# A written-out order of tasks, laid out anew: the first two layers of an attention and expert kernel, and which elementwise work GpSimd takes

## The chip, the cores and the metric

The kernel runs on one core of one Trainium2 chip. The metric is device time in microseconds of one execution, the median of several. The core's engines each run their own queue of instructions in order: PE (TensorE, matmuls; PEld is its loading of weights), DVE (VectorE), ACT (ScalarE), POOL (GpSimd), and SP (SyncE), which here only issues DMAs. An instruction whose input is not ready holds up everything behind it on its engine.

## The reference, cut to what matters

```python
# batch 4, heads 8, sequence 576, head width 64, 32 memory slots; all float32
a = softmax over the sequence of phi                      # (b, h, s, m)
k_m, v_m = a^T k, a^T v                                   # 32 memory rows per head
attn = softmax over m of (q k_m^T / 8)
x = (attn v_m), heads side by side                        # 2304 tokens x 512
h = x @ w_in                                              # 512 -> 2048
x = (max(h, 0) + alpha * min(h, 0)) @ w_out               # 2048 -> 512
p = domain_probs / (their sum + 1e-9)                     # 4 experts
out = sum over e of p[:, e] * (max(x @ w1[e], 0) @ w2[e]) # 512 -> 1024 -> 512
```

The weights w_in and w_out come as float64 and are decoded on the chip. "The first layers" below are the attention and the layer of w_in and w_out; the experts follow.

## The kernel before, in words

**Stages.** The attention of a batch `b` has two halves `g` of the heads (tasks `a{b}{g}_...`: the softmax of phi, its transposes on PE, the memory products, the scores, and their way back from PSUM) and a second softmax (`s{b}{g}{offset}_...`, class `Soft`, L364): `max`, `sub`, `exp`, `sum`, `mul`, `back`, then a split into a high and a low part, `hi` and `lo`. Batch 0 does it in two pieces of 288 columns, the others in one of 576. Then come 128 steps j of the first dense layer (class `First`, L542): for each of four blocks of 512 hidden columns, each batch, each half of 288 tokens, four pieces of 128 hidden columns. A step's tasks are `u{j}` (the up product on PE, L559 or L562), `n{j}` (two activations on ACT, L575 and L576), `v{j}` (DVE, L581), `h{j}` and `l{j}` (split into a high part on ACT, L585, and a low part, L232 on DVE or POOL), `d{j}` (the down product on PE, L597 or L600), and after four steps `e{j}` (the sum in PSUM goes to SBUF, L611 or L613). The first eight steps (batch 0, first block) are in plain float32 and have no `h` and `l`; the rest makes three float32r products of the high and low parts. `f{b}{c}{e}` folds the values of the attention into a piece of w_in on PE (L523), `fh` and `fl` split the result.

**Weights.** A block of w_in or w_out (`in{i}`, `out{i}`, class `Decode`, L442) is loaded into one of three buffers and decoded in steps: `_0` (DVE, L459), `_1` (ACT, L463), `_2` (DVE, L469 and L470), `_3` (L477, always DVE here), `_4` (the add, L496, DVE or POOL) and, for `out`, `_5` and `_6` (high part on ACT, low part on DVE or POOL, L232). The task `_3` also issues the load of a later block on SP (L438). SP's other loads, `p{b}`, `q{b}`, `kv{b}`, are tasks too, so their place in the order is their place in the queue of transfers. `w{i}` are idle matmuls that fill PE's early gaps.

**What sets the order.** The text ORDER names all tasks of the first layers in one sequence. They are issued in it, each to its own engine's queue; nothing is reordered afterwards, and the waits between engines follow from the data. The set ON_VECTOR names the tasks whose elementwise operation goes to DVE rather than POOL. `Soft` asks it once for both `sub` and `mul` (under the name of `sub`), and once for `lo`:

```python
 228     def engine(name):
 229         return nc.vector if name in ON_VECTOR else nc.gpsimd
...
 372         def views(self):
 373             s = pe_t[self.b][:, S2 + self.g * S + self.o:S2 + self.g * S + self.o + self.n]
...
 382         def sub(self):
 383             s, s3, shape = self.views()
 384             mx = self.mx
 385             self.eng.tensor_tensor(out=s3, in0=s3, in1=mx.to_broadcast(shape), op=ALU.subtract)
...
 399         def mul(self):
 400             s, s3, shape = self.views()
 401             rs = self.rs
 402             self.eng.tensor_tensor(out=s3, in0=s3, in1=rs.to_broadcast(shape), op=ALU.mult)
```

`Decode` asks it under `_3`, `_4` and, in the split, `_6`:

```python
 449 
 450         def open(self):
...
 472         def third(self):
 473             s = self.s.bitcast(F32)
 474             if self.eng is nc.gpsimd:
 475                 nc.gpsimd.tensor_tensor(out=s, in0=self.low.bitcast(F32), in1=s, op=ALU.mult)
 476             else:
 477                 nc.vector.scalar_tensor_tensor(out=s, in0=self.low, scalar=2.0**-52, in1=s, op0=ALU.mult, op1=ALU.mult)
 478             if n_raw[0] < n_dense + 2:
 479                 load_raw()
```

After ORDER has run, `run_experts` (L844) issues the experts in loops over 32 units of block and batch, by a fixed program that the change does not touch. Its first DMAs are the loads of the gates, `p<-pd` (L719), which stand on SP behind the task `sp3` (a store of batch 3's result, L625).

Of the kernel before, what the change touches and what calls it, by code (L numbers as in the profile page):

```python
# [1108 lines left out]
```

## Time and profile before

| | |
|---|---|
| time, median of 3 runs (lowest, highest) | 1208.26 us (1206.77, 1208.98) |
| the profiled execution's own time | 1206.66 us |
| its span, first to last instruction | 1204.7 us |
| mean granted TensorE clock over the span | 0.990 |
| busy: PE / PEld / DVE / ACT / POOL | 1170.1 / 1123.2 / 782.4 / 468.0 / 420.2 us |
| first layers, about | 0 to 418 us |
| experts, about | 418 to 1205 us |

The profile is that of one execution. Busy times are averages over stages that differ, so they are read stage by stage: the busy time of the engines in windows of the span, then the chain of work that ended last (followed back from the end, at each step to what released it), then the groups of instructions with count and mean duration. The two numbers ahead of a row of the timeline are its start and its duration, and the square bracket at its end is the engine's idle time before it and what ended that.

### The profile page before, as it was taken

Reading aid. Unit: us, or ns where it says so; the run is one execution under the profiler, and the core shown is the slowest. Engines: PE = TensorE matmul, PEld = TensorE weight load, DVE = VectorE, ACT = ScalarE, POOL = GpSimd, SP = SyncE. Lnnn points to the kernel's source line nnn. Section 1 sums busy time; section 2 is a strip of 40 time slices with the busy share of each in tenths; the row PEclk is TensorE's granted clock in tenths of the full one; section 3 lists DMA queues with packets and bytes.
Section 4 is the critical chain, followed back from the end, with each engine's and each line's share of the span. In section 5 each row is a group of like instructions: output and inputs, shape, how many; then the busy total and the mean of one; then the engine's idle time right before and its main releaser. Section 6 shows DMA issues by size and latency. Waiting matters only on the chain.

```text
span 1204.7 us, 21401 instructions
## 1 busy us (share of the span) xinstructions
PE 1170.1 (97%) x8794; PEld 1123.2 (93%) x8794; DVE 782.4 (65%) x1433; ACT 468.0 (39%) x1017; POOL 420.2 (35%) x361
## 2 busy tenths in 40 slices
PE   7799999999999989999999999989999999999998
PEld 6478899998999989999999999989999999999998
DVE  6999997685457744555566566676456656656553
ACT  4557665545455533323232223233422223232320
POOL 2212111232000054444534435465443552553430
PEclk9899999999999999999999999989999999999999
DMA  9642122010000132111112111132112111111001
GB/s 376 250 160 83 54 87 71 19 53 18 1 1 1 56 97 92 55 54 53 46 48 69 37 54 36 64 124 75 53 47 62 54 46 45 58 41 63 36 29 70
DMA packets 22994, 82.46 MB, mean 68 GB/s; under 512 B 3312, under 2 KB 4336, under 8 KB 20976
## 3 DMA queue, kind: packets, MB, share of 16 engines
q1 hardware_dynamic: 22896, 81.09, 19.8%
...
## 4 chain that ended last, share of the span: by engine, by line
PE 87%; DVE 9%; DMA 2%; ACT 1%; issue 1%; SPq 0%; ACTq 0%; DVEq 0%
PE o L823 34%; PE y L600 14%; PE uy L732 12%; PE uw L732 8%; PE ux L732 8%; PE h L562 7%; PE pw L523 2%; DMA rawin<-in_w_in 2%; PE y L597 1%; DVE g L232 1%; DVE xt L660 1%; DVE pos L581 1%; DMA p<-pd 1%; DVE min L469 0%; DVE mout L469 0%
## 5 line engine op out<-in xcount | busy, mean ns | idle before, releaser
L823 PE MATMUL o<-g,w 128*128 128x288 f32 x3072 | 450.9, 296 | 1.1 <-DVE g L232 1.1
L823 PEld LDWEIGHTS o<-g,w 128*128 128x128 f32 x3072 | 423.2, 189 | 1.8 <-DVE g L232 1.6
L232 POOL TENSOR_TENSOR w<-raww,w 128x512 fp32r<-128x512 f32 (+1 forms) x96 | 150.3, 1580 | 260.4 <-ACT w L507 155.3
L835 DVE TENSOR_TENSOR acc<-o,acc 128x288 f32<-128x288 f32 x224 | 102.1, 456 | 189.0 <-PE o L823 189.0
L600 PE MATMUL y<-g,wout 128*128 128x288 f32 x1440 | 210.1, 298 | 2.6 <-DVE g L232 1.0
L600 PEld LDWEIGHTS y<-g,wout 128*128 128x128 f32 x1440 | 195.9, 188 | 12.6 <-ACT pos L576 4.2
L732 PE MATMUL uy<-x,w 128*128 128x288 f32 x1152 | 186.0, 297 | 8.0 <-DVE v L766 8.0
L732 PEld LDWEIGHTS uy<-x,w 128*128 128x128 f32 x1152 | 164.7, 189 | 9.4 <-DVE v L766 9.3
L770 ACT COPY v<-ux 128x288 f32<-128x288 f32 x64 | 25.6, 400 | 291.8 <-PE ux L732 288.5
L801 ACT CAST g<-h 128x576 fp32r<-128x576 f32 x128 | 83.3, 676 | 139.5 <-DVE h L795 139.5
L232 POOL TENSOR_TENSOR g<-h,g 128x576 fp32r<-128x576 f32 x64 | 92.8, 1451 | 127.8 <-ACT g L801 123.0
L732 PE MATMUL ux<-x,w 128*128 128x288 f32 x768 | 123.4, 296 | 2.5 <-ACT v L770 2.5
L732 PE MATMUL uw<-x,w 128*128 128x288 f32 x768 | 123.1, 296 | 0.1
L795 DVE SCALAR_TENSOR_TENSOR h<-h,p 128x576 f32<-128x576 f32 x128 | 109.4, 855 | 6.4 <-DMA p<-pd 3.3
L562 PE MATMUL h<-a,wp 128*128 128x288 f32 x720 | 111.6, 297 | 0.3
L732 PEld LDWEIGHTS ux<-x,w 128*128 128x128 f32 x768 | 109.3, 189 | 2.7 <-ACT v L770 2.7
L732 PEld LDWEIGHTS uw<-x,w 128*128 128x128 f32 x768 | 109.3, 189 | 0.3 <-DVE y L611 0.3
L562 PEld LDWEIGHTS h<-a,wp 128*128 128x128 f32 x720 | 100.0, 188 | 5.3 <-issue 3.0
L766 DVE TENSOR_TENSOR v<-uy,v 128x288 f32<-128x288 f32 x128 | 58.5, 457 | 69.9 <-PE uy L732 69.4
L581 DVE SCALAR_TENSOR_TENSOR pos<-neg,nal,pos 128x288 f32<-128x288 f32 x120 | 64.7, 542 | 58.3 <-ACT pos L576 57.8
L575 ACT ACTIVATE neg<-h 128x288 f32<-128x288 f32 x128 | 52.8, 413 | 83.1 <-PE h L562 76.3
L232 POOL TENSOR_TENSOR g<-pos,g 128x288 fp32r<-128x288 f32 x24 | 19.7, 823 | 182.7 <-ACT g L585 134.2
(116 smaller groups left out, 1184.3 us busy)
## 6 DMA issues: line engine op xcount, KB each, us to landing
...
```

The lines of the kernel that those rows point to most:

```text
L232: eng.tensor_tensor(out=out, in0=in0, in1=in1.bitcast(F32), op=ALU.subtract)
L562: mm(p, wp_t[b, c, f // 2][:, x, o2 + g * 256:o2 + g * 256 + 128], a_t[b][:, y, g, o:o + HB], start=(n == 0), stop=(n == 5))
L575: nc.scalar.activation(out=neg, in_=p, func=AF.Relu, scale=-1.0)
L581: nc.vector.scalar_tensor_tensor(out=pos, in0=neg, scalar=nal[:, ft:ft + 1], in1=pos, op0=ALU.mult, op1=ALU.add)
L600: mm(First.acc[d], w[:, x, d * 128:(d + 1) * 128], self.gt[:, y, 0:HB], start=(self.start and n == 0), stop=(self.stop and n == 2))
L732: mm(p, w[:, x, a, k], operand(self.b, i)[:, y, k], start=(start and n == 0), stop=(n == 5), skip_group_check=not start)
L766: nc.vector.tensor_tensor(out=out, in0=x, in1=y, op=ALU.add)
L770: nc.scalar.copy(out=self.v1_t, in_=self.x)
L795: nc.vector.scalar_tensor_tensor(out=h, in0=h, scalar=0.0, in1=p_t[self.g // 2, self.b], op0=ALU.max, op1=ALU.mult)
L801: nc.scalar.copy(out=g_t[self.g, self.b, self.hp][:, i, 0], in_=h)
L823: mm(self.p, w[:, x, i, d % 2 * 128:(d % 2 + 1) * 128], g, start=(m == 0), stop=(m == 11))
L835: nc.vector.tensor_tensor(out=a, in0=self.p, in1=a, op=ALU.add)
```

## The change

It replaces the text of ORDER and the set ON_VECTOR. No task's own work is changed. The weights' adds of the first blocks, and other halves of the second softmax, go to POOL; other `lo`, `_4`, `_6` and `l` tasks change engine in either direction. The loads of `q1`, `p2` and `kv2` change place among the weights' loads. The numbers of idle matmuls change, and the fifth group (`w4`) is gone. Cut below: ORDER from its start until past step 24, and its end; ON_VECTOR whole.

```diff
 ORDER = """
-w0 p0 pal ppr kv0 pr0 pr1 pr2 q0 w1 p1 kv1 q1 a00_max a01_max a00_exp a01_exp a00_nat a00_sum a00_natc a01_nat a01_sum
-  pgates a01_nath a01_natc w2 a01_nathc a01_mem in0_1 in0_0 a00_mem in0_2 a01_memc in1_1 in0_3 out0_1 in1_0 in1_2
-  a01_memt a00_memc q01 p2 a01_memtc a00_memt out0_0 in1_3 a01_sc0 a00_memtc out0_2 q2 a00_sc0 a01_ev0 in0_4 w3 a00_ev0
-  s010_max in1_4 s000_max s010_sub f000 a10_max s000_sub s010_exp a11_max w4 fh000 out0_3 s000_exp a10_exp s010_sum
-  out0_4 a11_exp s000_sum a10_nat s010_mul a10_sum a10_natc a11_nat s000_mul s010_back a11_nath a11_natc a11_sum
-  a11_nathc s000_back in2_1 u0 out0_5 in2_0 u1 n0 in2_2 a00_sc1 n1 in2_3 a01_sc1 v0 in2_4 in3_1 d0
-v1 in3_0 in3_2 in3_3 in3_4 a01_ev1 out0_6 out1_1 a00_ev1 f001 s01288_max out1_0 out2_1 a10_mem out1_2 fh001 out3_1
-  out1_3 s000_hi out1_4 u2 a10_memc kv2 out2_0 d1
-n2 out2_2 out1_5 out2_3 s010_hi a11_mem s00288_max in4_1 out2_4 out3_0 out2_5 v2 s00288_sub d2
-s01288_sub s00288_exp out3_2 s01288_exp a11_memc out1_6 s00288_sum u3 s01288_sum a10_memt out2_6 n3 a20_max a11_memt
-  a10_memtc out3_3 a11_memtc a10_sc1 a20_exp s00288_mul p3 s01288_mul a10_sc0 out3_4 in5_1 v3 out3_5 s010_lo s01288_back
-  d3
-s00288_back s01288_hi out3_6 s00288_hi a10_ev0 s000_lo in6_1 u4 a10_ev1 e3 s01288_lo a11_sc1 s00288_lo s100_max s100_sub
-  n4 a11_sc0 a11_ev1 s100_exp v4 u5 a11_ev0 d4
-s110_max n5 s110_sub s100_sum s110_exp u6 f100 v5 n6 s110_sum d5
-fh100 s100_mul s110_mul u7 s100_back f101 q3 v6 s100_hi s110_back n7 d6
-pst s100_lo s110_hi fl100 fh101 s110_lo a20_nat a21_max u8 v7 a21_exp u9 fl101 d7
-n8 a20_sum a21_sum a20_natc v8 n9 in4_0 a21_nat h8 v9 a21_nath e7 l8 u10 in4_2 a21_natc d8
-in4_3 a21_nathc in5_0 h9 in5_2 a20_mem n10 l9 v10 in5_3 h10 a21_mem l10 a20_memc in6_0 a31_max in4_4 a31_exp in6_2 d9
-kv3 a21_memc in5_4 a30_max in7_1 u11 a31_sum a30_exp in6_3 a20_memt n11 a30_sum in6_4 a21_memt a20_memtc d10
-a21_memtc v11 out4_1 in7_0 a20_sc0 h11 in7_2 a20_sc1 a20_ev0 l11 u12 a20_ev1 s200_max a21_sc1 n12 s200_sub a21_sc0
-  a21_ev1 s200_exp v12 d11
-out5_1 a21_ev0 h12 s210_max l12 u13 s200_sum e11 s210_sub u14 d12
-n13 s200_mul s210_exp v13 f200 s210_sum h13 n14 l13 u15 s200_back fh200 s210_mul d13
-fl200 s200_hi n15 v14 f201 s200_lo s210_back h14 s210_hi a30_nat l14 a30_natc s210_lo d14
-fh201 v15 fl201 h15 u16 l15 in7_3 d15
-n16 out4_0 v16 out4_2 a31_nat h16 e15 a31_nath l16 u17 out4_3 a31_natc d16
-out5_0 in7_4 a31_nathc n17 out4_4 a30_mem out4_5 v17 out5_2 h17 out6_1 l17 out5_3 a31_mem a30_memc out4_6 out6_0 out7_1
-  out5_4 out6_2 u18 a31_memc d17
-n18 out6_3 out5_5 v18 u19 h18 out5_6 a30_memt l18 n19 out7_0 a31_memt a30_memtc v19 d18
-a31_memtc out6_4 h19 out7_2 out6_5 a30_sc1 in8_1 l19 out7_3 a30_sc0 a30_ev1 out6_6 u20 a30_ev0 s300_max out7_4 a31_sc0
-  n20 in9_1 a31_sc1 a31_ev0 out7_5 s300_sub d19
-a31_ev1 out7_6 s300_exp s310_max u21 v20 e19 s310_sub u22 s300_sum f300 h20 n21 l20 f301 s310_exp v21 h21 d20
-s310_sum n22 l21 fh300 s300_mul d21
-fh301 s310_mul in10_1 s300_back u23 v22 s300_hi s310_back h22 s300_lo s310_hi l22 n23 s310_lo d22
-fl300 v23 u24 fl301 h23 n24 u25 l23 in8_0 d23
-n25 v24 in8_2 h24 u26 e23 l24 v25 u27 in8_3 d24
-h25 in9_0 n26 l25 in9_2 n27 d25
...
-x1l1 n124 x1h2 v124 u125 h124 e123 l124 n125 u126 n126 d124
-v125 x1l2 h125 l125 u127 v126 d125
-n127 h126 v127 x1h5 l126 h127 d126
-x1l5 x1h6 l127 to wh01 x1l6 d127
+w0 p0 pal ppr kv0 pr0 pr1 pr2 w1 q0 p1 kv1 a01_max q01 a00_max a01_exp a00_exp a01_nat a01_sum pgates a00_nat a00_sum
+  a01_natc a01_nath a00_natc w2 a01_nathc a01_mem in0_1 in0_0 in0_2 a00_mem a01_memc in1_1 in1_0 out0_1 in1_2 a01_memt
+  a00_memc in0_3 a01_memtc a00_memt out0_0 a01_sc0 a00_memtc in1_3 a00_sc0 a01_ev0 in0_4 w3 a00_ev0 q1 s010_max p2
+  s000_max kv2 s010_sub a11_max s000_sub a10_max s010_exp a11_exp s010_sum in1_4 s000_exp a11_nat a10_exp s010_mul
+  s000_sum f000 s010_back a11_natc s000_mul a10_nat a11_sum fh000 a11_nath s000_back a10_natc out0_2 u0 a11_nathc
+  a01_sc1 out0_3 n0 a00_sc1 a01_ev1 out0_4 in2_1 u1 q2 a00_ev1 s01288_max in3_1 in2_0 a11_mem n1 s00288_max s01288_sub
+  a10_sum s00288_sub s01288_exp in2_2 s00288_exp a10_mem a11_memc in3_0 out0_5 in3_2 a11_memt a10_memc in2_3 a11_memtc
+  a10_memt s00288_sum in2_4 a11_sc1 a10_memtc s01288_sum a11_sc0 s00288_mul a10_sc1 a11_ev0 a10_sc0 v0 in3_3 s00288_back
+  s01288_mul a10_ev1 in3_4 s01288_back d0
+a11_ev1 out1_1 v1 out1_0 s000_hi f001 out1_2 s010_hi s00288_hi fh001 out1_3 s01288_hi u2 out1_4 out0_6 s110_max u3
+  out2_1 a10_ev0 n2 d1
+out2_0 out3_1 out2_2 n3 out2_3 u4 out1_5 v2 in4_1 u5 out2_4 n4 out3_0 d2
+out2_5 out3_2 out3_3 u6 in5_1 out3_4 p3 v3 f100 out3_5 v4 n5 s100_max s110_sub d3
+n6 a21_max v5 s110_exp s100_sub u7 e3 v6 out1_6 s110_sum f101 s100_exp a20_max out2_6 d4
+fh100 s100_sum n7 s110_mul fl100 a21_exp d5
+s100_mul a20_exp out3_6 s110_back fh101 s100_back d6
+pst in6_1 s01288_lo fl101 s100_hi v7 s110_hi s100_lo d7
+s110_lo a20_sum s00288_lo q3 a21_sum s000_lo u8 e7 s010_lo u9 in4_0 a20_nat in4_2 n8 a21_nat n9 u10 v8 in4_3 h8 a21_nath
+  a21_natc u11 l8 v9 n10 d8
+in5_0 a20_natc v10 a21_nathc in5_2 u12 h9 h10 a20_mem l9 l10 n11 in5_3 n12 v11 in6_0 a21_mem a20_memc v12 h11 in4_4
+  a30_max h12 a30_exp l11 a20_memt kv3 l12 d9
+a21_memc a30_sum in5_4 a20_memtc a31_max in7_1 a21_memt in6_2 a31_exp a20_sc0 u13 a20_ev0 a21_memtc a31_sum a20_sc1 n13
+  in6_3 a21_sc1 out4_1 a20_ev1 in6_4 u14 a21_ev1 s200_max a21_sc0 n14 d10
+s200_sub a21_ev0 s210_max a31_nat s210_sub s200_exp a30_nat v13 a31_natc d11
+s200_sum s210_exp a30_natc s210_sum s200_mul a31_nath e11 f200 s210_mul u15 a31_nathc v14 d12
+h13 s200_back h14 l13 s210_back fh200 l14 a31_mem n15 fl200 s200_hi v15 s210_hi s200_lo a30_mem a31_memc s210_lo h15
+  in7_0 out5_1 l15 in7_2 a31_memt a30_memc u16 out4_0 a31_memtc u17 n16 out4_2 a30_memt n17 a31_sc0 v16 a30_memtc d13
+v17 h16 a31_ev0 l16 in7_3 a30_sc1 h17 a30_sc0 l17 a30_ev1 a31_sc1 a30_ev0 in7_4 f201 s300_max a31_ev1 s300_sub d14
+fh201 s310_max fl201 s300_exp d15
+s310_sub out6_1 s300_sum s310_exp u18 e15 s310_sum s300_mul u19 f300 s310_mul n18 d16
+s300_back n19 v18 s300_hi v19 u20 h18 s310_back s300_lo h19 d17
+s310_hi l18 fh300 l19 u21 n20 s310_lo d18
+n21 v20 fl300 h20 u22 l20 v21 d19
+out4_3 h21 n22 l21 out4_4 u23 e19 v22 u24 out5_0 out6_0 f301 out5_2 h22 n23 d20
+l22 fh301 v23 n24 fl301 d21
+h23 v24 out4_5 l23 out5_3 h24 u25 l24 d22
+n25 out4_6 out5_4 out7_1 v25 u26 out5_5 out6_2 h25 u27 n26 d23
+l25 n27 v26 out6_3 h26 u28 e23 l26 u29 v27 out6_4 f010 out5_6 h27 n28 d24
...
+l124 h125 x1l5 x1h6 l125 u126 e123 u127 n126 n127 v126 d124
+x1l6 h126 x1h1 v127 d125
+l126 h127 x1l1 x1h2 l127 to wh01 d126
+x1l2 d127
 wl01 e127 sp3
 """
 ON_VECTOR = set("""
-in0_3 in10_3 in11_3 in12_3 in12_4 in13_3 in14_3 in15_3 in15_4 in1_3 in1_4 in2_3 in2_4 in3_3 in3_4 in4_3 in5_3 in6_3
-in7_3 in7_4 in8_3 in8_4 in9_3 in9_4 l10 l101 l102 l103 l105 l106 l107 l109 l110 l111 l112 l113 l114 l115 l116 l117 l118
-l119 l120 l121 l122 l123 l125 l126 l127 l14 l15 l16 l17 l18 l19 l20 l22 l23 l24 l25 l26 l27 l28 l29 l30 l31 l32 l33 l34
-l35 l36 l37 l38 l39 l41 l42 l43 l44 l47 l48 l50 l51 l52 l54 l55 l57 l58 l59 l60 l64 l65 l66 l67 l69 l70 l71 l72 l73 l74
-l75 l76 l77 l78 l8 l81 l82 l83 l85 l86 l87 l89 l9 l90 l91 l93 l94 l95 l97 l98 l99 out0_3 out10_3 out10_4 out11_3 out11_4
-out11_6 out12_3 out12_4 out13_3 out13_4 out14_3 out14_6 out15_3 out15_4 out1_3 out1_4 out2_3 out2_4 out3_3 out3_4 out3_6
-out4_3 out4_4 out4_6 out5_3 out5_4 out5_6 out6_3 out6_4 out7_3 out8_3 out8_6 out9_3 out9_6 s00288_mul s00288_sub
-s01288_lo s01288_mul s01288_sub s100_lo s100_mul s100_sub s110_lo s110_mul s110_sub s200_mul s200_sub s210_lo s300_lo
-s300_mul s300_sub s310_lo s310_mul s310_sub
+in0_3 in10_3 in11_3 in11_4 in12_3 in13_3 in13_4 in14_3 in15_3 in1_3 in2_3 in3_3 in4_3 in5_3 in6_3 in7_3 in8_3 in9_3
+in9_4 l10 l100 l101 l104 l105 l106 l108 l109 l11 l111 l112 l113 l114 l115 l118 l119 l12 l120 l121 l122 l123 l124 l126
+l127 l15 l16 l18 l19 l20 l21 l22 l23 l24 l25 l26 l27 l28 l29 l30 l31 l32 l33 l34 l35 l36 l37 l39 l41 l43 l44 l45 l47 l48
+l49 l51 l53 l56 l57 l59 l63 l64 l65 l68 l69 l70 l71 l72 l73 l74 l75 l76 l77 l78 l79 l8 l82 l84 l85 l86 l87 l88 l89 l9
+l91 l92 l93 l94 l95 l96 l97 l98 out0_3 out10_3 out11_3 out11_4 out11_6 out12_3 out12_4 out12_6 out13_3 out13_4 out13_6
+out14_3 out14_4 out15_3 out15_4 out15_6 out1_3 out1_4 out2_3 out2_4 out3_3 out3_4 out4_3 out4_4 out4_6 out5_3 out5_4
+out5_6 out6_3 out6_4 out6_6 out7_3 out7_4 out7_6 out8_3 out8_4 out9_3 out9_4 s010_lo s100_lo s100_sub s110_lo s200_lo
+s210_lo s210_sub s310_lo s310_sub
 """.split())
...
-    for i, n in enumerate((11, 12, 5, 5, 8)):
+    for i, n in enumerate((11, 12, 6, 13)):
```

## Rows read from the trace of the kernel before

**Rows 1.** The page, part 1: busy time, share of the span, instructions.
```profile
PE 1170.1 (97%) x8794; PEld 1123.2 (93%) x8794; DVE 782.4 (65%) x1433; ACT 468.0 (39%) x1017; POOL 420.2 (35%) x361
```

**Rows 2.** Windows; columns PE, PEld, DVE, ACT, POOL busy, granted clock, DMA share, GB/s.
```profile
0.00:140.00 140.00, 121.27 (x988) 95.28 (x989) 124.24 (x248) 83.40 (x213) 29.49 (x36) 0.96 0.51 191
...
74.00:140.00 66.00, 60.58 (x549) 50.92 (x548) 64.06 (x121) 45.26 (x123) 15.87 (x13) 1.00 0.29 101
140.00:400.00 260.00, 259.15 (x1915) 241.44 (x1914) 185.65 (x374) 139.06 (x351) 40.20 (x39) 1.00 0.11 33
400.00:440.00 40.00, 36.23 (x253) 34.72 (x252) 25.06 (x49) 18.90 (x42) 9.34 (x7) 0.96 0.29 101
```

**Rows 3.** The chain that ended last, 75 to 150 us, and a step at 440.
```profile
74.67 0.52 DVE pos L581
...
134.50 1.73 PE y L600 x11
...
439.82 1.60 PE o L823 x12
```

**Rows 4.** Groups of PE, 74 to 140 us: count, busy us, mean ns, idle before.
```profile
L600 PE MATMUL y<-g,wout 128*128 128x288 f32 x192 | 29.8, 302 | 1.9 <-ACT g L585 0.9 <-DVE g L232 0.7 <-POOL g L232 0.2
L562 PE MATMUL h<-a,wp 128*128 128x288 f32 x102 | 16.4, 300 | 0.0
L325 PE MATMUL pm<-kv,pe 128*32 128x128 f32 (+1 forms) x160 | 5.6, 277 | 0.0
```

**Rows 5.** Timeline, 20 to 33 us: POOL operations and what DVE does beside them.
```profile
20.66 1.59 POOL L385 TENSOR_TENSOR pe<-pe,mx 128x288 f32<-128x288 f32 x2 [4.27 <-DVE mx L379]
21.00 0.45 DVE L379 TENSOR_REDUCE mx<-pe 128x9 f32<-128x288 f32 x1
...
29.49 1.27 POOL L232 TENSOR_TENSOR wout<-wholeout,wout 128x512 fp32r<-128x512 f32 x1 [2.59 <-ACT wout L500]
...
29.67 1.37 DVE L470 TENSOR_SCALAR sin<-min 128x512 uint32<-128x512 uint32 x1
```

**Rows 6.** Groups of the whole trace: the second softmax's `sub` and `mul`.
```profile
L385 DVE TENSOR_TENSOR pe<-pe,mx 128x576 f32<-128x576 f32 (+1 forms) x7 | 5.8, 833 | 0.1
...
L402 DVE TENSOR_TENSOR pe<-pe,rs 128x576 f32<-128x576 f32 (+1 forms) x7 | 4.3, 649 | 0.0
...
L385 POOL TENSOR_TENSOR pe<-pe,mx 128x288 f32<-128x288 f32 (+1 forms) x3 | 2.8, 931 | 4.3 <-DVE mx L379 4.3
L402 POOL TENSOR_TENSOR pe<-pe,rs 128x288 f32<-128x288 f32 (+1 forms) x3 | 2.5, 835 | 1.3 <-DVE rs L396 0.9 <-DVE sm L287 0.4
```

**Rows 7.** Groups by shape, DVE and POOL, 0 to 140 us.
```profile
L469 DVE SCALAR_TENSOR_TENSOR min<-min,sin 128x512 uint32<-128x512 uint32 x9 | 8.0, 893 | 0.9 <-ACT min L463 0.6
L232 DVE TENSOR_TENSOR g<-pos,g 128x288 fp32r<-128x288 f32 x13 | 7.3, 564 | 0.0
...
L477 DVE SCALAR_TENSOR_TENSOR sout<-rawout,sout 128x512 f32<-128x512 uint32 x8 | 5.5, 685 | 0.1
L469 DVE SCALAR_TENSOR_TENSOR mout<-mout,sout 128x512 uint32<-128x512 uint32 x8 | 5.5, 685 | 0.2
L470 DVE TENSOR_SCALAR sin<-min 128x512 uint32<-128x512 uint32 x9 | 5.3, 585 | 0.3
...
L470 DVE TENSOR_SCALAR sout<-mout 128x512 uint32<-128x512 uint32 x8 | 3.4, 427 | 0.3
...
L496 DVE TENSOR_TENSOR win<-min,sin 128x512 f32<-128x512 f32 x4 | 2.7, 684 | 0.0
...
L496 POOL TENSOR_TENSOR win<-min,sin 128x512 f32<-128x512 f32 x4 | 5.4, 1355 | 40.8 <-DVE sin L477 36.9 <-DVE sm L287 3.9
```

**Rows 8.** Timeline, 36 to 38 us: the landing of the load of `out1`, and its first use on DVE.
```profile
36.43 0.67 ACT L463 ACTIVATE mout<-rawout 128x512 f32<-128x512 f32 x1 [3.42 <-DMA rawout<-in_w_out]
...
37.29 0.41 DVE L459 TENSOR_SCALAR sout<-rawout 128x512 uint32<-128x512 uint32 x1
```

**Rows 9.** The chain that ended last, 400 to 442 us: into the experts.
```profile
417.82 2.02 DVE w L232
...
421.70 6.51 DMA p<-pd
```

More of the change, by code (lines that the diff above doesn't have):

```diff
@@ L169 @@
-x1t3 v123 x1h4 h123 d122
-x1l4 l123 u124 x1h1 d123
-x1l1 n124 x1h2 v124 u125 h124 e123 l124 n125 u126 n126 d124
-v125 x1l2 h125 l125 u127 v126 d125
-n127 h126 v127 x1h5 l126 h127 d126
-x1l5 x1h6 l127 to wh01 x1l6 d127
+w0 p0 pal ppr kv0 pr0 pr1 pr2 w1 q0 p1 kv1 a01_max q01 a00_max a01_exp a00_exp a01_nat a01_sum pgates a00_nat a00_sum
[7 more added lines that the diff above has]
+  s01288_mul a10_ev1 in3_4 s01288_back d0
@@ new lines @@
+l27 out7_0 n29 v28 d25
+v29 h28 fh010 l28 out6_5 fl010 d26
+h29 out7_2 in8_1 l29 u30 out7_3 d27
+n30 out6_6 in9_1 v30 u31 out7_4 e27 in8_0 u32 in8_2 f011 h30 n31 l30 d28
+in9_0 n32 v31 in9_2 h31 d29
+fh011 l31 out7_5 v32 u33 out7_6 h32 d30
+n33 l32 fl011 in10_1 v33 u34 in8_3 h33 d31
+l33 n34 in9_3 v34 u35 e31 in10_0 u36 in10_2 f110 n36 in10_3 d32
+h34 v36 fh110 l34 in8_4 n35 fl110 d33
+h36 v35 in11_1 l36 u37 h35 in9_4 u38 l35 n37 in11_0 d34
+n38 v37 in11_2 h37 out8_1 d35
+l37 v38 out8_0 h38 u39 e35 in10_4 u40 n39 l38 f111 out9_1 v39 n40 d36
@@ new lines @@
+out11_6 h51 v52 fh310 l51 u53 h52 fl310 in14_1 l52 u54 n53 in12_0 d49
+n54 v53 in12_2 u55 h53 l53 d50
+v54 n55 in13_0 v55 d51
+h54 in13_2 l54 u56 h55 e51 l55 u57 n56 f311 n57 v56 in12_3 d52
+fh311 v57 fl311 in12_4 d53
+h56 l56 in13_3 d54
+h57 in14_0 l57 in15_1 in14_2 u58 d55
+in13_4 n58 in14_3 v58 u59 e55 in14_4 h58 u60 n59 f020 l58 out12_1 v59 n60 d56
+in15_0 h59 v60 fh020 l59 d57
+h60 fl020 out13_1 l60 u61 in15_2 d58
+n61 out12_0 out12_2 u62 v61 d59
+n62 in15_3 h61 v62 u63 l61 e59 h62 u64 l62 n63 f021 n64 v63 out12_3 h63 d60
@@ new lines @@
+fh021 l63 v64 fl021 in15_4 d61
+h64 l64 out14_1 u65 out13_0 out12_4 d62
+n65 out13_2 out12_5 u66 v65 out13_3 h65 u67 n66 l65 d63
+out12_6 n67 v66 v67 h66 u68 e63 h67 l66 u69 out15_1 l67 n68 f120 out14_0 n69 v68 d64
+out13_4 fh120 v69 out13_5 fl120 d65
+h69 out14_2 d66
+h68 l69 l68 out14_3 u70 out13_6 d67
+out15_0 n70 out14_4 v70 out14_5 u71 e67 h70 out14_6 u72 n71 f121 l70 v71 n72 u73 out15_2 h71 d68
+fh121 l71 fl121 n73 d69
+v72 v73 h72 out15_3 u74 h73 l72 l73 u75 n74 out15_4 d70
+n75 ws00 out15_5 d71
@@ new lines @@
+u76 e71 u77 f220 v74 d72
+v75 h74 out15_6 wopen h75 fh220 l74 d73
+l75 n76 fl220 n77 v76 d74
+h76 v77 wh00 l76 d75
+h77 wl00 u78 e75 u79 n78 f221 l77 v78 n79 d76
+ws01 h78 fh221 d77
+fl221 u80 u81 f320 l78 v79 n80 d78
+h79 v80 fh320 l79 u82 h80 fl320 n81 d79
+l80 v81 n82 u83 e79 h81 u84 l81 f321 n83 v82 h82 d80
+v83 fh321 l82 h83 fl321 n84 l83 u85 u86 v84 n85 d81
+h84 v85 l84 n86 d82
+h85 v86 l85 d83
+h86 l86 u87 e83 u88 n87 f030 n88 v87 h87 d84
+v88 fh030 l87 fl030 d85
+h88 l88 d86
+d87
+u89 e87 u90 n89 f031 n90 v89 h89 d88
@@ new lines @@
+v90 fh031 l89 h90 fl031 u91 l90 u92 n91 d89
+n92 v91 h91 v92 u93 l91 h92 u94 l92 n93 d90
+n94 v93 h93 v94 d91
+l93 h94 l94 u95 e91 u96 n95 f130 n96 v95 h95 d92
+v96 fh130 l95 fl130 d93
+h96 l96 u97 u98 n97 d94
+n98 v97 h97 v98 u99 l97 h98 d95
+l98 n99 v99 u100 e95 h99 u101 l99 n100 f131 n101 v100 d96
+v101 fh131 fl131 d97
+h100 l100 d98
+h101 l101 u102 u103 n102 d99
+n103 v102 h102 v103 u104 l102 e99 h103 u105 l103 n104 f230 n105 v104 d100
+fh230 v105 fl230 d101
+h105 l105 d102
+h104 l104 u106 u107 n106 d103
@@ new lines @@
+n107 v106 h106 v107 u108 l106 h107 e103 u109 l107 n108 f231 n109 v108 d104
+v109 fh231 x0t0 x0h0 fl231 d105
+h109 x0t1 x0h2 l109 x0h3 d106
+x0t2 h108 x0h1 l108 x0t3 u110 x0l1 d107
+n110 x0l3 v110 u111 e107 h110 u112 l110 n111 f330 n112 v111 x0l0 d108
+h111 fh330 l111 v112 x0h6 fl330 d109
+h112 l112 x0l6 u113 x0l2 x0h4 d110
+n113 x0l4 x0h5 v113 d111
+h113 x0l5 l113 u114 e111 u115 n114 f331 n115 v114 x1t0 h114 d112
+fh331 l114 v115 x1h0 fl331 d113
+h115 l115 x1t1 d114
+x1t2 x1l0 u116 x1t3 u117 n116 d115
```

116 lines of the change are left out of this document (20 added, 96 removed).

## The prediction

> **What bounds the kernel now.** I read the page's busy times first. PE is busy 97% of the span [rows 1], so all its idle time together is 1204.7 - 1170.1 = 34.6 us: no order of issue can gain more than a few per cent. The windows show where that time lies [rows 2]. From 140 to 400 us PE is busy 259.15 of 260 while DVE is busy 185.65 (71%): PE sets the pace, and DVE work that moves into this stretch is hidden there. From 74 to 140 it is the other way round: DVE is busy 64.06 of 66. The chain says the same: from the `pos` at 74.67 to 134.50 nearly all its links are DVE's, and from the down product at 134.50 on they are PE's [rows 3]. So the change is worth what it does to DVE's queue before about 135 us, and the start, which waits for transfers, stays.
>
> What the stretch from 74 to 140 costs PE I count from its instructions, since the ends of matmuls are modelled and a busy PE may be a waiting one. Twelve matmuls of 128x288 take 1.60 us where nothing holds them up, 0.133 each [rows 3]. The 192 of L600 and 102 of L562 are then 39.2 us, not the 46.2 they show; the 160 records of L325 take 5.6 [rows 4]; the folds, scores and transposes of that stretch come to some 13 to 15 more in the same view. That is 58 to 60 of 66 us: **6 to 8 us are lost** there, and I take 7.
>
> **The part that removes DVE work.** I count the instructions that the two orders issue ahead of step 24's down product (`d24`), which runs at about 141 us before. On DVE the new order has, ahead of that point:
> - 4 `sub` and 4 `mul` of the second softmax fewer (two pieces of 288 columns, two of 576): 4 x 0.833 + 4 x 0.649 = 5.9 us [rows 6];
> - 4 adds `_4` of w_in fewer: 4 x 0.684 = 2.7 [rows 7];
> - 2 blocks of w_out decoded later: each `_0` (taken as long as L470), `_2` and `_3`, 0.427 + 0.685 + 0.427 + 0.685 = 2.2, so 4.4; and one low part `_6`, same shape as the add, 0.7 [rows 7];
> - 2 `v` and 3 `l` more, as steps run a little further ahead: 5 x 0.564 = 2.8 [rows 7].
>
> Together DVE has 5.9 + 2.7 + 4.4 + 0.7 - 2.8 = **11 us less** to do. On POOL the same softmax work is 4 x 0.931 + 4 x 0.835 = 7.1 [rows 6] and 4 adds are 4 x 1.355 = 5.4 [rows 7]; two other 128x512 operations (2.7) and one `l` (taken at 0.8) leave it. POOL has **9 us more**, and it is busy 29.49 of the first 140 [rows 2], so it has the room. PE has 12 up matmuls, a fold and an idle matmul more ahead of `d24`: 12 x 0.133 + 1.0 + 0.1 = 2.7 us that it need not do later.
>
> **What POOL's work costs DVE.** It is not free. POOL's subtract at 29.49 runs 1.27 us, and the `TENSOR_SCALAR` that DVE starts at 29.67 takes 1.37, ending just after it, instead of the 0.427 of its undisturbed form [rows 5, 7]. A reduction is not held: 0.45 us at 21.00, in the middle of POOL's 20.66 to 22.25 [rows 5]. In the first 140 us the groups hold 9 x (0.893 - 0.685) = 1.9 us of such stretching for L469 and 9 x (0.585 - 0.427) = 1.4 for L470 [rows 7]; read the same way, the seven other groups that are stretched (L232, L289, L395, L459 and L581) bring it to about 12. POOL's own work in that time is 29.49 less 1.3 of memsets, 28.2 [rows 2]. So a POOL microsecond has cost DVE 12/28.2 = 0.43. The bounds are 0 (POOL beside reductions and transposes alone) and 1 (DVE always waits). I take 0.43, since much of the same kind of work stands beside it: 9 x 0.43 = 3.9 us. DVE's queue is then 11 - 3.9 = 7.1 us shorter at `d24`, and with PE 2.7 us further ahead that is worth **9.8 us** if DVE alone decides.
>
> The Trainium skill (SBUF - State Buffer, section "SBUF: two separate sides") calls the port pair of the two engines an exclusive lock: whichever starts first keeps it for its whole instruction, and the other waits. Its GPSIMD Engine Reference (section 4.1, "Engine selection") says to keep elementwise work on a tile on VectorE, as GpSimd is about twice slower with two inputs. Rows 5 agree with the first for `TENSOR_SCALAR`, and 1.355 against 0.684 in rows 7 with the second; by the lock taken at its worst, 1:1, the sum would be the second rival below.
>
> **What PE allows.** Counted the same way ahead of `d7` (73 us before), DVE loses 8.6 us, POOL gains 9.0 (3.9 on DVE), and PE has 1.9 less to do: 8.6 - 3.9 - 1.9 = 2.8 us gained by then. With the 7 of the stretch after it, PE can get back 9.8 at most: both limits agree. Where two engines are nearly full each makes the other wait: DVE, the bound, stood idle 1.9 of the 66 us [rows 2]. I give PE the same, leaving 9.8 - 1.9 = **7.9 us**.
>
> **Loads.** `q1`, `p2` and `kv2` now stand on SP ahead of the load of `out1`, where `q1`, the rest of `q0`, `p2` and `q2` stood. That is 1152 KB more, 1.18 MB; 191 GB/s at a busy share of 0.51 is 375 GB/s when busy [rows 2], so 3.1 us. `out1` landed at 36.4 and DVE took it up at 37.3 [rows 8]; now it should land at about 39.5. DVE's work ahead of its first use, counted as above, is 28 us; with 10 of the 13.9 us that DVE stands idle before 74 (140 - 124.24, less the 1.9 after 74 [rows 2]) and 10 us of POOL's work at 0.43 it is due at about 42. `in2` and `in3` land a little earlier, with `q1` behind them. I cost both at nothing, covered by that queue; uncovered, at up to 3 us.
>
> **The end of the first layers.** The loads of the gates on SP wait for `sp3`, that for `e127`, and `e127` stands on DVE behind the low part of the experts' first weights, 417.82 to 419.84 (2.02 us); the gates need 6.51 us from 421.70, and PE loses 40 - 36.23 = 3.8 us around it [rows 2, 9]. In the new order the last `n` stands four down products ahead of the end rather than three, so that chain starts 1.6 us earlier against PE. Bounds 0 and 1.4 (no further than `e127`'s own wait for PE); I take 0.4, as the chain has other links.
>
> **Sum.** 7.9 + 0.4 = 8.3 us. The profiled execution's 1206.66 (span 1204.7 and 2.0 around it) would become 1198.4; it lies 1.6 below the median of 1208.26, which would become **1200.0**.
>
> **Rivals.** Second: the lock at 1:1. Then DVE gains 11 - 9 = 2 and PE 2.7; less the 1.9 of friction, plus 0.4, the time is 1208.26 - 3.2 = 1205.1. For it: nearly all softmax work on POOL falls beside decoding, whose operations are the ones held. Against it: DVE's reductions and transposes stand there too.
>
> Third, slower: the softmax's round trips. DVE's `sum` waits for `exp`, that for a `sub` now on POOL, and `back` for a `mul` on POOL; DVE is in order, so if the next names in ORDER are not ready, it stands. The work there is 4 + 4 operations of 288 columns and 3 + 3 of 576; at rows 6's means 7 x 0.931 + 7 x 0.835 = 12.4 us. If DVE stands for all of it, it has 11 - 3.9 - 12.4 = -5.3, with PE's 2.7 and the friction -4.5, so about 1212.4. It turns to slower once over (9.8 - 1.9)/12.4 = 64% of these times stand open. Against it: the new order puts two halves side by side and other blocks' decoding between.
>
> Fourth: no difference. The stretch regains its 7 us, but PE loses them to new waits for low parts and `v` that come just in time, as both queues are full until step 40: 2.8 - 1.9 = 0.9 is left, about 1207.4. For it: PE and DVE would have nearly equal work there. Against it: from 140 on PE lost only 0.85 us in 260 beside a DVE at 71% [rows 2].
>
> **How the numbers follow.** Forecast 0.56, second 0.16, third 0.14, fourth 0.14. Even the forecast's good end is limited: 9.8 + 1.4 = 11.2 without friction, 1197, and some 4 us more if DVE's idle time at the start shrinks from its 13.9, 1193. The range reaches from there to 1208.5 and leaves out most of the third rival and a little below. A measurement of this kernel can tell about 0.2%, 2.4 us, from no change. Faster by more than that (under 1205.8): the forecast and most of the second, 0.71. Within: the rest of the second and the fourth, 0.16. Slower: 0.13.
>
> **What would show it.** In the windows, 74 to 140 us should show PE nearer to full and DVE still near 64, with POOL well over 16; the chain should pass from DVE to PE well before 134 us, for good. L469, L470 and their like should have longer means than in rows 7; means near 1 us would favour the second rival. Idle DVE ahead of L394 or L408 with POOL as releaser would show the third. If PE's idle time before 74 us grows by more than 3 us, or `e127`, at 419.84 before, comes later than 414 us, I am wrong.

## The result, and the profile after

Four runs of the changed kernel have a median of **1190.79 us** (1190.35 to 1191.59); beside them the kernel before took 1207.7. The ratio is 0.986 [0.9843, 0.9877]: 16.9 us faster, where 8.3 were forecast, and below the range. The profiled executions lie 14.9 us apart (span 1189.8 against 1204.7); the one of before was the lowest of its runs and the one of after the highest of its own, which is the other 2 us. The traces have to account for 14.9.

The page of the changed kernel, part 1, answers to [rows 1]:

```profile
PE 1161.6 (98%) x8796; PEld 1117.0 (94%) x8796; DVE 775.7 (65%) x1419; ACT 466.3 (39%) x1017; POOL 432.4 (36%) x375
```

The windows of the changed kernel, columns and stretches as in [rows 2]:

```profile
0.00:140.00 140.00, 128.32 (x1061) 102.86 (x1062) 121.27 (x244) 86.89 (x225) 37.24 (x45) 0.98 0.51 187
74.00:140.00 66.00, 64.63 (x592) 55.47 (x591) 60.01 (x121) 45.51 (x123) 12.69 (x11) 1.00 0.27 91
240.00:280.00 40.00, 40.00 (x298) 36.53 (x297) 30.11 (x57) 20.98 (x52) 10.56 (x12) 1.00 0.09 27
400.00:440.00 40.00, 37.34 (x276) 36.41 (x275) 23.80 (x39) 16.88 (x33) 20.54 (x16) 1.00 0.25 85
```

And two windows of the kernel before that the rows ahead of the prediction lack:

```profile
240.00:280.00 40.00, 39.24 (x286) 35.48 (x286) 32.81 (x59) 20.51 (x49) 14.10 (x13) 1.00 0.18 53
430.20:433.60 3.40, 3.24 (x12) 2.89 (x12) 0.60 (x3) 2.11 (x4) 3.34 (x3) 0.50 0.00 0
```

From 74 to 140 us PE runs 592 matmuls, not 549, and DVE is busy 60 of 66, not 64: it now has time to spare. Nearly all of POOL's growth stands ahead of 74 us: 37.24 - 12.69 = 24.6 us there, against 13.6 before. From 240 to 280 the busy time grows by only 0.76, but 12 more matmuls run, which is 1.6 us of work.

The chain that ended last in the changed kernel, from 93 us and into the experts, answers to [rows 3, 9]:

```profile
95.55 0.49 DVE pos L581
...
102.29 0.60 DVE sin L477
103.34 0.71 PE pc L357 x4
104.05 0.86 PE pw L523 x8
104.91 3.37 PE y L600 x24
...
404.37 2.11 DVE w L232
406.48 1.47 DVE y L611 x4
...
408.34 6.18 DMA p<-pd
...
416.49 1.06 PE ux L732 x6
417.55 0.80 PE uy L732 x6
```

DVE leaves the chain at 103 us, 31 us sooner than before, and PE has it until 399, but for 0.8 us of ScalarE's at 379.

The signs that the prediction named came out in part: PE is nearer to full from 74 to 140 and the chain passes to it sooner, but DVE is not near 64 there, and POOL has 12.69 us, where "well over 16" was named.

To see where the time came from I use one count throughout. **PE's loss** at step j is the time at which `d`j starts, less all work that ORDER gives PE ahead of it, each kind of matmul at its undisturbed duration. A rise between two steps is time that PE lost there, whether the profile calls it idle or hides it in a long matmul. Last column: from the first matmul of the experts to their 150th.

```
us                    d0    d8   d24   d61  d127   first   to 150th
before              15.8  26.2  34.0  36.2  41.2  418.45   25.98
after               15.8  21.8  24.5  26.0  28.7  406.14   23.57
new order only      15.1  24.0  27.3  28.9  31.6  409.01   23.79
new engines only    17.5  25.7  36.7  39.4  45.2  422.49   25.25
```

Of the 14.9 us, 4.4 were won by `d8`, 5.1 more by `d24`, 3.0 from there to `d127` and 2.4 at the entry to the experts. The forecast had 7.9 for the first two together, nothing for the third and 0.4 for the fourth.

### The profile page after: what moved, and what is told of

It reads as the page before. It is cut to its first block, busy times and chain, and to the rows that moved or that the text cites. A ratio compares the mean times of both kernels' runs of the same rounds, so it can differ in the third digit from the quotient of the medians.

```text
span 1189.8 us, 21436 instructions
## 1 busy us (share of the span) xinstructions
PE 1161.6 (98%) x8796; PEld 1117.0 (94%) x8796; DVE 775.7 (65%) x1419; ACT 466.3 (39%) x1017; POOL 432.4 (36%) x375
## 4 chain that ended last, share of the span: by engine, by line
PE 89%; DVE 5%; DMA 3%; ACT 1%; issue 1%; POOL 0%; SPq 0%; DVEq 0%; POOLq 0%; ACTq 0%
PE o L823 33%; PE y L600 15%; PE uy L732 12%; PE ux L732 8%; PE uw L732 8%; PE h L562 8%; PE pw L523 2%; PE y L597 1%; DMA q<-in_q 1%; DMA rawout<-in_w_out 1%; DMA p<-pd 1%; PE pc L357 1%; DVE x L232 1%; DMA yu<-ysp 0%; DVE w L232 0%
## 5 line engine op out<-in xcount | busy, mean ns | idle before, releaser
L600 PE MATMUL y<-g,wout 128*128 128x288 f32 x1440 | 205.6, 297 | 0.0
L562 PE MATMUL h<-a,wp 128*128 128x288 f32 x720 | 108.8, 296 | 0.1
L232 POOL TENSOR_TENSOR g<-pos,g 128x288 fp32r<-128x288 f32 x29 | 24.3, 841 | 173.3 <-ACT g L585 143.1
```

The costliest lines, as they stand in the source:

```text
L232: eng.tensor_tensor(out=out, in0=in0, in1=in1.bitcast(F32), op=ALU.subtract)
L562: mm(p, wp_t[b, c, f // 2][:, x, o2 + g * 256:o2 + g * 256 + 128], a_t[b][:, y, g, o:o + HB], start=(n == 0), stop=(n == 5))
L600: mm(First.acc[d], w[:, x, d * 128:(d + 1) * 128], self.gt[:, y, 0:HB], start=(self.start and n == 0), stop=(self.stop and n == 2))
```

## The experiments

**Which stretch.** Four kernels take the new order, and its engines, in one stretch each and the old one elsewhere. The first edit below is the last kernel's, whole but for two `l` that change engine (`l124` to DVE, `l125` to POOL); of the other three the seams are shown.

```diff
-x1t3 v123 x1h4 h123 d122
-x1l4 l123 u124 x1h1 d123
-x1l1 n124 x1h2 v124 u125 h124 e123 l124 n125 u126 n126 d124
-v125 x1l2 h125 l125 u127 v126 d125
-n127 h126 v127 x1h5 l126 h127 d126
-x1l5 x1h6 l127 to wh01 x1l6 d127
+x1t3 x1h4 x1l4 v123 h123 u124 l123 u125 n124 d122
+n125 v124 h124 v125 x1h5 d123
+l124 h125 x1l5 x1h6 l125 u126 e123 u127 n126 n127 v126 d124
+x1l6 h126 x1h1 v127 d125
+l126 h127 x1l1 x1h2 l127 to wh01 d126
+x1l2 d127
```

```diff
-n8 a20_sum a21_sum a20_natc v8 n9 in4_0 a21_nat h8 v9 a21_nath e7 l8 u10 in4_2 a21_natc d8
+s110_lo a20_sum s00288_lo q3 a21_sum s000_lo u8 e7 s010_lo u9 in4_0 a20_nat in4_2 n8 a21_nat n9 u10 v8 in4_3 h8
+a21_nath a21_natc u11 l8 v9 n10 d8
...
 out5_1 a21_ev0 h12 s210_max l12 u13 s200_sum e11 s210_sub u14 d12
```

```diff
 n8 a20_sum a21_sum a20_natc v8 n9 in4_0 a21_nat h8 v9 a21_nath e7 l8 u10 in4_2 a21_natc d8
...
-out5_1 a21_ev0 h12 s210_max l12 u13 s200_sum e11 s210_sub u14 d12
+s200_sum s210_exp a30_natc s210_sum s200_mul a31_nath e11 f200 s210_mul u15 a31_nathc v14 d12
```

```diff
 fh021 v64 h63 fl021 out14_1 l63 d61
-h64 l64 out12_2 d62
-out12_3 out13_0 d63
+out12_2 out12_3 h64 l64 u65 out13_0 out12_4 d62
+n65 out13_2 out12_5 u66 v65 out13_3 h65 u67 n66 l65 d63
```

> The new order and engines up to step 8 (d8), the old ones from there on. Theory, the gains add up by stretch: at d8 the new trace is 4.4 us ahead for the same PE work, and that is kept, so about 4 to 5 us faster than before (ratio 0.996). Rival, the old order's DVE queue from step 8 to 24 still sets the pace and takes it back, as DVE has as much to do there as before: 0 to 2 us faster.

> The new order and engines only from step 8 to step 61. Theory, the gains add up: 5 to 6 us faster, what the new trace gains between these steps. Rival, DVE enters the stretch with the old start's backlog and the new middle cannot show its gain: under 3 us.

> The new order and engines only from step 61 to step 121, where PE sets the pace. What the prediction held: nothing to gain there, 0 us. Theory from the two traces: about 2 us faster, since short waits of PE for DVE and ACT between 248 and 275 us are gone.

> The new order only from step 121 to the end of the first layers. What the prediction held: 0.4 us faster. Theory from the two traces: 2 to 3 us faster; the gates' loads are issued 1 us earlier against PE's last down product, PE idles 1.4 instead of 2.5 us for them, and the granted clock after that idle time stays at 1.00 instead of falling to 0.83 for ten microseconds.

Measured: up to `d8` 1202.84, 0.9956 [0.9939, 0.9973]; `d9` to `d61` 1202.31, 0.9951 [0.9936, 0.9965]; `d62` to `d121` 1203.61, 0.9962 [0.9948, 0.9977]; the end 1205.12, 0.998 [0.9967, 0.9993], all against 1207.71. That is 4.9 + 5.4 + 4.1 + 2.6 = 17.0 us, the whole change: within their intervals, of 1.6 to 2 us either way each, the stretches add up, and no gain is seen to be given back later. The half after `d61`, which the forecast held for hidden, is worth 4.1 by the medians and some 2 by its trace (loss at `d127` 39.6 against 41.2).

**Order or engines.** One kernel has the new order with the old engines, another the old order with the new engines; a third is the changed kernel with the second softmax's seven other `sub` and `mul` pairs back on DVE. The first two edits are cut to the lines that tell the kernels apart; of the third the names that join ON_VECTOR are shown.

```diff
-w0 p0 pal ppr kv0 pr0 pr1 pr2 q0 w1 p1 kv1 q1 a00_max a01_max a00_exp a01_exp a00_nat a00_sum a00_natc a01_nat a01_sum
+w0 p0 pal ppr kv0 pr0 pr1 pr2 w1 q0 p1 kv1 a01_max q01 a00_max a01_exp a00_exp a01_nat a01_sum pgates a00_nat a00_sum
...
 in0_3 in10_3 in11_3 in12_3 in12_4 in13_3 in14_3 in15_3 in15_4 in1_3 in1_4 in2_3 in2_4 in3_3 in3_4 in4_3 in5_3 in6_3
```

```diff
 w0 p0 pal ppr kv0 pr0 pr1 pr2 q0 w1 p1 kv1 q1 a00_max a01_max a00_exp a01_exp a00_nat a00_sum a00_natc a01_nat a01_sum
...
-in0_3 in10_3 in11_3 in12_3 in12_4 in13_3 in14_3 in15_3 in15_4 in1_3 in1_4 in2_3 in2_4 in3_3 in3_4 in4_3 in5_3 in6_3
+in0_3 in10_3 in11_3 in11_4 in12_3 in13_3 in13_4 in14_3 in15_3 in1_3 in2_3 in3_3 in4_3 in5_3 in6_3 in7_3 in8_3 in9_3
```

```diff
+s000_sub s00288_sub s010_sub s01288_sub s110_sub s200_sub s300_sub
```

> The new order with the old choice of engines. Theory, DVE's queue: ahead of d24 the new order then keeps about 5.9 us of softmax work and 2.7 of adds on DVE that the change takes away, and POOL's holding of DVE falls by some 4; at least half of the gain up to step 24 is lost, so 7 to 11 us faster than before. Rival, the order makes nearly all of it: 14 us or more.

> The old order with the new choice of engines. Theory: DVE has about 8.6 us less to do up to d24 and is held 4 us more, so 3 to 5 us faster. Rival, the order was laid out for its own engines and POOL's longer operations now stand in DVE's chains: 0 or slower.

> The new kernel with every sub and mul of the second softmax on DVE (seven pieces come back to it: 10.3 us of DVE work more, 12.4 of POOL's less). At my price of 0.43 DVE's queue up to step 24 grows by 10.3 - 5.3 = 5 us: 3 to 5 us slower than the new kernel. If POOL holds DVE 1:1, it shrinks by 2: no slower. If POOL costs DVE nothing: 8 to 10 us slower.

Measured: order alone 1195.51, 0.9898 [0.9883, 0.9913]; engines alone 1210.24, 1.0022 [1.0008, 1.0035], slower; the softmax back on DVE 1195.49, 0.99 [0.9885, 0.9914]. Order is worth 13.0 us by itself, the engines nothing by themselves, and some 4 on top of the new order, which is as much as the softmax's share alone loses when it goes back. ("Order" is that of all queues: it also puts 12 up matmuls more ahead of `d24` on PE, and moves ScalarE's work and the loads.)

Part of why the same engines cost time in the old order shows in DVE's list of waits from 20 to 140 us. First the kernel with the new engines only (line, releaser, us in total, times, longest; its lines stand 6 further down), then two lines of the kernel before:

```profile
DVE a L238 <- ACT a L421: 2.1, 2, 1.4
DVE pe L368 <- PE pc L363: 1.9, 1, 1.9
DVE g L587 <- ACT g L582: 1.3, 1, 1.3
```

```profile
DVE pe L362 <- PE pc L357: 1.7, 1, 1.7
...
DVE a L232 <- ACT a L415: 0.8, 1, 0.8
```

I count DVE's work up to `l24` with each instruction at the lower quartile of its form (same line, operation and shape). This kernel then has 6.8 us less of it than before (117.0 against 123.8). But DVE's instructions run 18.0 us beyond that, against 12.7, and DVE idles 19.0 us against 15.7. 6.8 - 5.3 - 3.3 = -1.8, nearly the 2.6 us by which `l24` ends later (142.4 against 139.8); the records of DVE overlap in part, so the sum does not close. The larger part is the hold, by which I mean the stretching of DVE's instructions beside POOL's. What DVE idled for were ScalarE and PE: no line of the list is a `sum` (L400 here) or a `back` (L414) that waits for the softmax's own results.

**What gives the slack.** I read how long before `d`j starts `l`j, the last thing that it needs, is finished (by DVE; `l80` by POOL in both kernels):

```
us from the end of l to the start of d:    16     24     32     80
before                                   0.12   1.00   1.38   0.32
after                                    8.51   8.34   7.42   4.85
new order only                           8.88   8.34
new engines only                        -0.61   1.00
```

(Where a number is negative, PE starts on parts that are ready.) Not every step differs so: at step 48 it is 6.75 before and 7.14 after. If this lead is what shields PE, then more work on DVE should cost little in the new order and all of it in the old. Two kernels carry seven idle reductions of 0.74 us on DVE, 5.2 in all, behind `v16` to `v22`; a third has them behind `v2` to `v8` of the new order. The outputs don't depend on them.

```diff
+    still = const.tile([128, S], F32, name="still")
+    top = const.tile([128, 1], F32, name="top")
...
+    for i in range(7):
+        task(f"busy{i}", nc.vector.tensor_reduce, top, still, AX.X, ALU.max)
```

> The new kernel with seven idle reductions of 128x576 on DVE (0.74 us each, 5.2 in all), one behind each of v16 to v22. Theory, lead: from step 16 on each step's low part is done 8 us before PE takes it, so DVE is not the bound there, and the 5.2 us cost under 1 us. Rival, what I forecast: DVE and PE are both near full until step 32, and at least 3 us of it show.

> The kernel before with the same seven reductions behind its v16 to v22. Theory, DVE sets the pace there (each low part is done 0.1 to 1.2 us before PE takes it): 4 to 5.5 us slower than before. Rival, PE's waits there have another cause: under 2 us.

> The new kernel with the seven idle reductions on DVE (5.2 us) behind v2 to v8 instead of v16 to v22. Theory, DVE still sets the pace up to step 8 in the new kernel (v7 ends 0.06 us before d7): 4 to 5.5 us slower than the new kernel, against 2.2 for the later place. Rival, loads or PE set the pace there: under 3 us.

Measured: in the new order 1194.2, 0.9901 [0.9882, 0.992], beside 1192.03, 0.9883 [0.9864, 0.9903], of the unchanged new kernel: 2.2 us. In the old order 1213.45, 1.006 [1.0037, 1.0082]: 7.2 us, and the loss at `d24` is 39.9 instead of 34.0. Near the start of the new order 1196.07, 0.992 [0.9892, 0.9948], which is 3.2 to 4.8 us more than the three kernels under "The start" below, and the loss at `d8` is 26.0 instead of 21.8. So DVE is the bound at these steps of the old order and near the start of the new one, and at steps 16 to 22 of the new one it costs PE less than half of the work put in. The 2.2 was more than I expected, and less than the rival's 3. Most of it is lost between `d12` and `d14` (2.0, against 0.3 in the unchanged kernel), and PE's waits up to 150 us name another consumer (lines 10 further down):

```profile
PE pc L367 <- DVE pe L372: 1.8, 2, 1.0
```

```profile
PE pc L357 <- DVE pe L362: 0.3, 1, 0.3
```

The first is the kernel with the reductions, the second the changed kernel. The scores of the next attention wait for DVE's transposes: a lead on `l` shields the down products, not the other work that PE takes from DVE. In PE's waits from 74 to 140 us of the kernel before, the same wait is the largest; behind it stand a transpose that waits for ScalarE, and the down products that wait for their high and low parts. After the change that list has the 1.0 of L342 and the 0.3 above, and nothing else:

```profile
PE pc L357 <- DVE pe L362: 2.2, 2, 1.2
PE pt L342 <- ACT kvb L332: 1.1, 1, 1.1
PE y L600 <- ACT g L585: 0.9, 2, 0.5
PE y L600 <- DVE g L232: 0.7, 1, 0.7
```

**The entry to the experts.** Two kernels issue the loads of the gates earlier on SP: ahead of `sp3`, and ahead of `wl01` and `e127`.

```diff
-wl01 e127 sp3
+wl01 e127 g0 g1 sp3
...
-        load_gates(0, 0)
-        load_gates(0, 1)
...
+    task("g0", load_gates, 0, 0)
+    task("g1", load_gates, 0, 1)
```

```diff
-wl01 e127 sp3
+g0 g1 wl01 e127 sp3
```

> The new kernel with the two first loads of the gates on SP ahead of the store sp3 (and so no longer behind the last e). Theory, they wait only for the store's turn: issued 2 us earlier and landing in 4 instead of 6.2 us, PE's idle 1.4 us before the experts' second group goes, 1.5 to 2.5 us faster than the new kernel. Rival, their tile's place comes free as late as before, or the transfer is no faster: no change.

> The new kernel with the two first loads of the gates on SP ahead of the experts' first weights too (task wl01), so not behind that load either. Theory: as with the loads ahead of sp3 alone, PE no longer waits for the gates, 1.5 to 2 us faster than the new kernel; nothing beyond that, since no wait is left there. Rival: SP stands for the tile's place and holds the weights' load behind it, slower than the new kernel.

Measured: 1189.15, 0.985 [0.9835, 0.9865], and **1188.03**, 0.9847 [0.9829, 0.9864] (1187.38 to 1188.55). The second is the fastest kernel of this study, 4.0 us under the 1192.03 of the new kernel beside it. The first 150 matmuls of its experts take 21.50 us, not 23.97: 2.5 us are the gates. The rest is the start, whose loss at `d0` is 14.6 here and between 14.6 and 17.3 in the other kernels of the new order, without a cause that I can name. The chain that ended last, in the second kernel, 398 to 423 us (its lines stand 6 further down):

```profile
398.49 6.35 PE y L606 x48
404.83 0.80 PE ux L738 x6
405.63 0.79 PE uy L738 x6
...
408.84 0.47 DVE v L772
...
421.56 1.60 PE o L829 x12
```

No transfer is left in this stretch of it, where the changed kernel has 6.18 us of one. The gates were known long before; the load stood on SP behind work that it has nothing to do with.

**The start.** Three kernels test what else could make it: `q1` moved back ahead of the attention, 5 and 5 idle matmuls for 6 and 13, and `kv2` behind the weights of the first blocks. Of a moved load its new place is shown; its old one, further on for `q1` and further ahead for `kv2`, is empty.

```diff
-w0 p0 pal ppr kv0 pr0 pr1 pr2 w1 q0 p1 kv1 a01_max q01 a00_max a01_exp a00_exp a01_nat a01_sum pgates a00_nat a00_sum
+w0 p0 pal ppr kv0 pr0 pr1 pr2 w1 q0 p1 kv1 q1 a01_max q01 a00_max a01_exp a00_exp a01_nat a01_sum pgates a00_nat
```

```diff
-    for i, n in enumerate((11, 12, 6, 13)):
+    for i, n in enumerate((11, 12, 5, 5)):
```

```diff
-out2_5 out3_2 out3_3 u6 in5_1 out3_4 p3 v3 f100 out3_5 v4 n5 s100_max s110_sub d3
+out2_5 out3_2 out3_3 kv2 u6 in5_1 out3_4 p3 v3 f100 out3_5 v4 n5 s100_max s110_sub d3
```

> The new kernel with the load q1 back in its old place on SP, ahead of the rest of q0 and of the weights in2 and in3, which then land 2.8 us later (about 30 and 31 us). Theory, the loads' new order is part of the early gain: 1.5 to 3 us slower than the new kernel. Rival, DVE's queue covers the loads, as I forecast: within 0.7 us of it.

> The new kernel with 5 and 5 idle matmuls in its third and fourth group as before, for 6 and 13. Theory, they keep the granted clock at its upper level between 30 and 50 us and nothing else: up to 1.5 us slower. Rival, they only fill a wait: no difference.

> The new kernel with the load kv2 moved on SP behind the loads of out1, out2 and out3, which then land 5.7 us earlier (out1 at about 35 instead of 40.5 us, where ACT stands 6.1 us for it). Theory, ACT's wait holds up the high parts and the activations behind it and so DVE and PE: 1 to 3 us faster than the new kernel. Rival, DVE's queue is the bound at that time and is busy through the wait: within 0.7 us.

Measured: 1192.85, 0.9882 [0.9856, 0.9908]; 1191.31, 0.9871 [0.9852, 0.9891]; 1191.76, 0.9875 [0.9855, 0.9895]. None differs from the new kernel (0.986 and 0.9883). The timeline of the changed kernel answers to [rows 8] and shows why a later landing cost nothing:

```profile
40.52 0.70 ACT L463 ACTIVATE mout<-rawout 128x512 f32<-128x512 f32 x1 [6.08 <-DMA rawout<-in_w_out]
41.70 0.41 DVE L459 TENSOR_SCALAR sout<-rawout 128x512 uint32<-128x512 uint32 x1
...
45.63 1.16 POOL L385 TENSOR_TENSOR pe<-pe,mx 128x576 f32<-128x576 f32 x1 [4.17 <-DVE mx L379]
45.80 1.27 DVE L459 TENSOR_SCALAR sout<-rawout 128x512 uint32<-128x512 uint32 x1
```

`out1` lands at 40.5, ACT stood 6.08 us for it, and DVE comes to it at 41.70 after other work. When `kv2` is moved, ScalarE takes `out1` up at 34.69 us without a wait, and the time does not fall. So neither `q1`'s place nor `kv2`'s nor the idle matmuls make the start's gain, each taken alone; `p2` and `q2` I did not move back. The reductions behind `v2` to `v8` show that DVE sets the pace there; which part of its new sequence saves the 4.4 us, I did not isolate.

## Why the prediction was wrong

The sign and the place were right: DVE's queue ahead of about 135 us was the bound, the change shortened it, and PE took over at 103 us for good. The size was half. By the traces 14.9 - 8.3 = 6.6 us were missed: 1.6 up to `d24` (9.5 where 7.9 stood), 3.0 from there to `d127` (where nothing stood) and 2.0 at the entry (2.4 where 0.4 stood). Step by step:

**DVE's work, "ahead of step 24's down product".** This is the first step that failed. I counted 11 us less ahead of `d24` in ORDER, and as a count that held (16 instructions, about 10 us). But PE doesn't wait for everything that stands ahead of `d24`; it waits for `l24`. Ahead of `l24` DVE has 17.1 us less (106.7 against 123.8; between 15.7 and 17.1 as the undisturbed durations are taken), 8.3 of them with the old engines, from order alone: the new order puts a step's `v` and `l` ahead of decoding and attention that nothing needs yet. A count up to the consumer is blind to that. Counted up to `l24`, DVE would have stood clear of the bound rather than level with PE, and the 1.9 of friction would have had no ground.

**The friction of 1.9.** It was taken because two engines would be nearly full side by side. With a lead of 8 us hardly any is left: the gain at `d24` is 9.5 against the 9.8 that the same step gave without friction. The split was off, though: 4.4 up to `d8`, where 2.8 were counted by `d7`, and 5.1 after it, where 7 were. PE's loss between `d8` and `d24` was 7.8 before (I had 6 to 8) and is 2.7 now, not 0.

**POOL's price of 0.43.** It held in size: DVE's instructions ahead of `l24` run 14.0 us over beside 36.5 of POOL's, 0.38, against 12.7 beside 28.5 before, 0.45. 1:1, the second rival, is ruled out as an average: at 1:1 the softmax's return to DVE would have cost nothing, and it cost some 4 us. My sign for the means in [rows 7] did not: the hold moved from one form to another, and the groups by shape of the changed kernel, 0 to 140 us, have L469 and one L470 free and the other L470 and L477 held:

```profile
L496 POOL TENSOR_TENSOR win<-min,sin 128x512 f32<-128x512 f32 x8 | 10.6, 1326 | 37.0 <-DVE sin L477 37.0
...
L477 DVE SCALAR_TENSOR_TENSOR sin<-rawin,sin 128x512 f32<-128x512 uint32 x8 | 6.5, 816 | 0.0
...
L469 DVE SCALAR_TENSOR_TENSOR min<-min,sin 128x512 uint32<-128x512 uint32 x8 | 5.5, 687 | 0.5 <-ACT min L463 0.3
...
L470 DVE TENSOR_SCALAR sout<-mout 128x512 uint32<-128x512 uint32 x8 | 5.4, 671 | 0.3
...
L470 DVE TENSOR_SCALAR sin<-min 128x512 uint32<-128x512 uint32 x8 | 3.4, 427 | 0.3
```

The price stands for a mix of work, though, and goes with the order more than with the engines: with the new engines in the old order it was 18.0 beside 38.9, 0.46, and with the old engines in the new one 9.0 beside 25.8, 0.35. The Trainium skill (SBUF — State Buffer, section "SBUF: two separate sides") limits the exclusive lock to vector operations of some kinds, those with two inputs in SBUF or in a two-port mode. That a reduction is not held [rows 5], and a mean well under 1:1, agree with it. L459, with one input in SBUF, is held in the timeline above (1.27 us behind the subtract of 45.63, instead of 0.41); in which mode it ran no run here shows.

**"140 to 400 nothing".** This is the second step that failed, and at 3.0 us the largest. I read it from PE's busy time, 259.15 of 260, though the prediction itself says that a busy PE may be a waiting one. Counted by work, PE lost 7.2 us between `d24` and `d127` before and 4.2 after. The window from 240 to 280 shows it: 0.76 us of idle time stood for 12 missing matmuls, 1.6 us. What goes with the gain is the lead: with the new order alone the rise is 4.3, and the kernel with the new order from `d62` to `d121` has its lead of 4.85 us at step 80 and gains there. That the lead makes it was not tested apart.

**The loads.** Right: `out1` landed at 40.5 (39.5 estimated) and was taken up at 41.7 (42), covered: its earlier landing in the last experiment gained nothing.

**The end, 0.4 with bounds 0 and 1.4.** This is the third step that failed: it was 2.4. Against the first matmul of the experts, `e127` came 1.05 us sooner, and PE's pause ended 1.4 us sooner: 416.49 - 406.14 = 10.35, against 430.19 - 418.45 = 11.74. That is the upper bound. What the bound left out is the clock, below: the first two groups behind the pause took 1.4 us more before. By the 150th matmul less of it is left. Two kernels with the old end show no fall of the clock there, the one with the new order from `d9` to `d61` and the one with the new engines only; their first 150 take 25.17 and 25.25 us, against 25.98 before. So some 0.8 of the 2.4 is the clock, and the rest the pause.

**The third rival** had only its sign, and only in the old order: 1.7 us slower. The idle DVE ahead of L394 or L408 that was to show it stands in no list of DVE's waits from 20 to 140 us, neither of the changed kernel nor of the one with the new engines only; there it was the hold, and waits for ScalarE and PE.
